# A new instruction order, and with it ten engine choices, for chunk-selected attention with a gated MLP on one core

## The chip, the cores and the metric

The kernel runs on one core of a Trainium2 chip. The metric is the device time of one execution in microseconds (us). The engines are TensorE (PE in the profile), VectorE (DVE), ScalarE (ACT), GpSimd (POOL) and SyncE (SP); the last one only issues DMA transfers here.

## The reference

```python
# attention, per head: q, k, v are [4, 8, 768, 64]
k_min, k_max = chunks_of_32(k).min(), chunks_of_32(k).max()        # 24 chunks
ub = sum_d max(q * k_min, q * k_max)                               # [768, 24]
ub = where(chunk(query) >= chunk, ub, -1e9)
top_chunks = argsort(ub)[..., -6:]                                 # six chunks per query
scores = where(in top_chunks and query >= key, q @ k.T / 8, -1e9)
x = softmax(scores) @ v                                            # heads joined: [4, 768, 512]
# gated MLP, per batch
h = gelu_tanh(x @ w_in)                                            # [768, 1024]
u, v = h[:, :512], h[:, 512:]
v = layernorm(v) * g_ln
v_s = w_sg @ v + b_sg                                              # along the 768 positions
out = x + (u * v_s) @ w_out
```

## The kernel before

The work is cut into 1374 named operations. A name is a kind, a number and, often, a part. Attention goes by pairs of heads, 0 to 15; a batch is four pairs; selection goes by pair for pairs 0 and 1, and by two pairs at a time after that. For each pair there are:

- loads `lk`, `lq`, `lv` (two each, SP, line 503);
- transposes by TensorE into PSUM, `kt` and `qt` (line 512), with reductions over chunks `kn` and `kx` (VectorE, line 530), the copies out of PSUM `ke`, `ka`, `kb` and `qe` (ScalarE at line 519 or VectorE at line 521), the difference `kw` (VectorE or GpSimd, line 541) and the rectified query `qr` (VectorE at line 562, ScalarE at line 564);
- casts `qc`, `qa`, `qb`, `vc` on GpSimd;
- selection: bounds `ub` on TensorE, then `ut`, `uc`, `um`, `ud`, `uq` on VectorE, and for the later pairs the small transfers `d` on SP (line 658);
- per head: scores `s` on TensorE, exponentials `e` on ScalarE (lines 736 and 770), the causal cut `af` on GpSimd (line 672), products with the values `pv` and `pd` on TensorE, the reciprocal `xr` on VectorE (line 804), and the scaled copy `xs`, as one VectorE instruction (line 813) or six ScalarE instructions (line 810);
- the transpose `xt`, by TensorE with a copy `xe` for some, by a DMA transpose on SP for the others.

For each batch the MLP has `hv` and `hu` on TensorE (lines 853 and 900) with their activations `gv` and `gu` on ScalarE, statistics `bs` and `ba` and small helpers `re`, `rm` on VectorE and `rp`, `rn` on GpSimd, the normalisation `vh` (ScalarE at line 886, VectorE at line 891), the product along positions `pt` (TensorE, line 920), its scaling `vs` (VectorE, line 927), the gating `gm` (GpSimd or VectorE, line 933), the output product `ou` (TensorE, line 943), the sum with x `oa` (VectorE, line 950) and the store `os` (SP). There are three result buffers for `oa` and `os`. The weights come in through `win`, `wsg`, `wo`, and `wt` with `we` transposes one of them.

The order is a table written out in the file, `ORDER`. Each engine takes its operations in the order in which they stand in the table and runs strictly in that order; `@` behind a name chooses the other engine that the operation allows; `:` gives the PSUM buffers. PSUM has two buffers of 1024 columns for scores and four of 512 for everything else. Waits are derived from the table: an operation waits for those that it depends on, and for the readers of the buffer that it overwrites. At most six large loads are in flight (`WINDOW`). `FILL` names TensorE operations that are preceded by so many matmuls of zeros while they wait for their PSUM buffer's readers or their inputs. The `cost` figures are the planner's durations in nanoseconds; nothing that runs depends on them.

Of the kernel before, what the change touches and what calls it, by code (L numbers as in the profile page):

```python
# [6 lines left out]
ALU = mybir.AluOpType  # L7
# [11 lines left out]
J0 lk1.1 warm0 zA2 lk1.0 zB3 lk0.1 idF zB1 J lk0.0 W01 Jn lq0.1 lq0.0 kt1.0:0 kt1.1:1 kn1.0 lq2.0 vx10 W00 kn1.1 lq1.0  # L19
kx1.1 kt0.0:2 kt0.1:3 kx1.0 ke1.1 lq1.1 kn0.0 ke1.0 kn0.1 lq2.1 qt0.1:1 kx0.1 qt0.0:0 qe0.1 kx0.0 lk2.0 qe0.0 vx12  # L20
qr0.1 kw0@pool kw1@pool qr0.0@act zB2 lk2.1 IND ke0.0 ke0.1 ub0:10 iA0 lk4.0 qt1.0:2 ut0.0 qc0 qt1.1:3 ut0.1 lk4.1
qe1.0 uc0.00 uc0.10 qe1.1 uc0.01 uc0.11 uc0.02 uc0.12 um0.0 lq3.1 qr1.1@act qc1 qt2.1:1 um0.1 qr1.0@act qt2.0:0 qe2.1
ud0.0 lq3.0 qe2.0 ub1:32 ud0.1 uq0.0 iB2 qr2@act uq0.1 lk3.0 W02 kt2.1:1 ut1.0 qc2 s0.4:0 ut1.1 uc1.00 s0.2:1 kn2.1
lk3.1 e0.4 idB uc1.10 uc1.01 kx2.1 s0.3:0 e0.2 lv0.1 uc1.02 uc1.11 um1.0 kt4.1:0 e0.3 uc1.12 kt2.0:3 W03 lv0.0 um1.1
s0.5:1 kn2.0 ke2.1 af1.1 lq4.0 e0.5 kx2.0 s0.0:0 iA1 ke2.0@dve lq4.1 qt3.0:2 e0.0 qt3.1:1 kn4.1 s0.6:1 ud1.1 lq5.1
ud1.0 qe3.0 kt3.0:3 uq1.1 af1.0 e0.6 s0.1:0 uq1.0 lk5.0 vc0 kn3.0 kt3.1:2 e0.1 kx4.1 s1.0:1 qe3.1 af0.0 lk5.1 kx3.0
ka4.1 s1.1:0 af1.2 kn3.1 ke3.0 af0.2 pv1:1 lv1.1 kb4.1@dve kw2@pool e1.1 af0.1 pd1 pv0:3 kx3.1 e1.0 zA0 lv1.0 qt4.1:0
xr1 xs1 pd0 s1.5:0 qe4.1 af3.0 lq5.0 xr0 ke3.1 xs0 kt4.0:1 qr3@act zA3 vx13 vx11 qt4.0:0 lv3.1 kw3@pool kn4.0 af2.0
xt0.0:2 qe4.0 s1.3:1 qc3 xe0.0 e1.5 lq6.0 kx4.0 kt5.0:3 zA1 ub2:02 e1.3 kn5.0 lk6.0 kw4@pool af2.2 af3.2 kx5.0 vc1
ka4.0 lv2.1 s1.2:0 ut2.0 kb4.0 ut2.1 s1.6:1 lk6.1 e1.2 uc2.00 uc2.10 qt5.1:0 um2.0 qt5.0:1 lq6.1 e1.6 af3.1 um2.1  # L30
s1.4:0 qe5.0 af2.1 kt5.1:2 lk7.1 e1.4 ud2.0 qe5.1 ud2.1 ka5.0 pv2:1 lk7.0 uq2.0 pv3:0 qr5@act uq2.1 pd2 kb5.0 lv2.0
pd3 kn5.1 s2.0:1 qr4@act xr3 kx5.1 lq7.0 xs3 s2.5:0 e2.0 xr2 ka5.1@dve kt6.1:3 lq7.1 qt6.1:0 e2.5 xs2 wsg0 s2.3:1 kw5
lv3.0 kb5.1 kn6.1 qa4 s2.2:0 e2.3 kx6.1 ub4:12 win0 ka6.1@dve qe6.1 iA2 e2.2 s2.4:1 ut4.0 kb6.1 wsg5 ut4.1 s2.1:0 e2.4
uc4.00 vc2 um4.0 xt0.1:0 e2.1 qt7.1:1 wsg2 ud4.0 kt6.0:3 qe7.1@dve s3.4:1 xe0.1@act af5.0 uq4.0 s3.5:0 kn6.0 e3.4
d4.01 af4.0 kt7.0:2 kx6.0 d4.00 qt7.0:1 e3.5 kn7.0 qt6.0:0 win1 d5.00 s3.1:1 ka6.0@dve qe7.0 iB0 d5.01 qe6.0@dve
s3.3:0 e3.1 kb6.0@dve wsg3 pv5:1 kw6 e3.3 kx7.0 nh wt0:0 win3 s3.0:1 ka7.0@dve vc3 qr7@act pv4:3 we0 e3.0 qa5 pd5
kb7.0@dve s3.2:0 xr5 kt7.1:0 e3.2 win2 xs5 gln pd4 s8h.2:1 qr6@act xr4 af6.0 wt2:2 lq9.1 kn7.1 s8h.1:0 e8h.2 xs4 lq8.1
pv6:1 af7.0 e8h.1 we2 lq8.0 pd6 wt5:3 kx7.1 lq9.0 s10h.0:1 we5 ka7.1 kw7@pool pv7:2 qa6 xr6 kb7.1 pd7 xs6 xt0.2:3
e10h.0 qb6 xr7 s10h.1:0 uc4.10 xs7 ub6:01 e10h.1 zB0 xt0.3:2 qb5 ut6.0 xe0.2@act s8h.0:1 xe0.3 s10h.2:0 wo2 e8h.0
um4.1 wt3:0 hv0.1:3 wsg4 uc6.00 lv4.0 ud4.1 e10h.2 we3 qb4 hv0.3:2 uq4.1 ut6.1 iA3 hv0.0:0 d4.11 um6.0 d4.10 gv0.1  # L40
hv0.2:1 wsg1 gv0.0 lk8.0 bs0.1 af8.0 hu0.00:3 gv0.3 d5.10 ba0.1 bs0.0 gv0.2 iB3 qt8.1:0 lv5.0 hu0.30:2 gu0.00 bs0.3
lk8.1 qe8.1 qb7 qt8.0:1 ba0.3 d5.11 gu0.30 ba0.0 hv0.5:3 bs0.2 qe8.0 bsg hv0.4:0 ba0.2 lk10.0 gv0.5 re0.0 ud6.0 rp0.0
qr8@act bs0.5 hu0.31:2 gv0.4 uq6.0 qt9.1:1 gu0.31 rm0.0 hu0.20:3 uc6.10 bs0.4 rn0.0 qe9.1 iB1 hu0.10:0 lv5.1 vh0.1
ba0.5 ba0.4 re0.1 rm0.1 gu0.20 rp0.1 wt1:2 vh0.0 s9h.0:1 lv4.1 we1 gu0.10 hu0.21:1 rn0.1 vh0.2 vh0.4@dve lk9.1
hu0.11:3 gu0.21 vh0.3@dve d6.01 vh0.5 hu0.01:2 um6.1 d6.00 gu0.11 kt8.1:0 gu0.01 ud6.1 wt4:1 s11h.0:0 we4 lq10.1
pt0.01:3 kn8.1 kx8.1 lk10.1 e11h.0 pt0.02:2 vs0.01 vc5 lk9.0 e9h.0 uq6.1 pt0.00:1 vs0.02 d6.10 wo3 ka8.1 d7.00 s9h.1:0
gm0.02 vs0.00 kt8.0:3 d6.11 e9h.1 qt9.0:2 kn8.0 vc4 s9h.2:1 lk11.1 pt0.03:1 qe9.0@dve e9h.2 lv8.0 wo0 kx8.0 kb8.1
d7.01 s11h.1:0 wo1 gm0.00@dve ka8.0 s11h.2:1 lq12.1 af9.0 pv8:2 vs0.03 qr9@act lv6.0 pv9:0 e11h.1 af10.0 pd8 pt0.11:1
xr8 kb8.0@dve e11h.2 af11.0 lq12.0 s12h.0:0 vs0.11 qa7 pd9 pt0.12:3 e12h.0 lv6.1 xr9 gm0.03@dve d7.10 xs9@act s13h.1:1
kw8 s13h.0:0 vs0.12 gm0.01 xs8@act pv10:1 gm0.12@dve kt9.0:0 e13h.0 pt0.10:3 kn9.0 gm0.11 lv7.0 e13h.1 kx9.0 d7.11  # L50
pd10 s12h.2:0 qb8 vs0.10 pv11:2 ka9.0 lq10.0 xr10 pd11 e12h.2 kb9.0@dve s14h.0:1 xt1.0 gm0.10 ou0.2:3 xr11 xs10@act
af13.0 e14h.0 lv7.1 s13h.2:0 oa0.2 kt9.1:0 vc6 ou0.1:1 kn9.1 xs11@act s12h.1:1 e13h.2 oa0.1 pt0.13:3 e12h.1 kx9.1
os0.1 s14h.1:0 kw9@pool lq11.0 af12.0 ka9.1 vs0.13 kt10.1:2 lq11.1 e14h.1 s15h.0:1 kn10.1 gm0.13 pv13:1 os0.2 kb9.1
pv12:3 lv8.1 qa9 e15h.0 pd12 pd13 lk11.0 s14h.2:0 xr13 vc7 ou0.0:0 xr12 kx10.1 e14h.2 xs13 af15.0 ka10.1 s15h.1:1 xs12
s15h.2:0 kb10.1 af14.0 oa0.0 ou0.5:1 xt1.2 e15h.2 qa8 ou0.4:3 e15h.1 oa0.5 xt1.1 pv14:2 oa0.4 pd14 pv15:0 xr14 os0.0
xs14@act pd15 qt11.1:1 xr15 qt11.0:3 xs15 qe11.1 qe11.0 kt11.1:2 xt1.3 kt10.0:0 kn11.1 qt10.1:1 ou0.3:3 kx11.1 qe10.1
lv9.1 kn10.0 ka11.1 lv10.0 qt10.0:1 oa0.3 kb11.1 qe10.0 kx10.0 kt11.0:2 ka10.0 kw10@pool ub8:31 kn11.0 lk14.1 qb9
kb10.0 kx11.0 vc8 hv1.1:0 ut8.0 uc8.00 ut8.1 lv11.0 qb10 hv1.0:3 gv1.1 um8.0 os0.5 ka11.0 qb11 hv1.2:1 bs1.1 lk12.1
gv1.0 lq13.0 uc8.10 ud8.0 kb11.0 hv1.3:0 ba1.1 lv9.0 uq8.0 gv1.2 bs1.0 hv1.4:3 lv11.1 qr11@act um8.1 d9.01 gv1.3
hu1.00:2 ba1.0 gv1.4 bs1.2 lk12.0 hu1.20:1 qr10@act ud8.1 d9.00 qt12.1:0 gu1.00 bs1.3 hu1.01:3 os0.3 qe12.1 ba1.2  # L60
gu1.20 hv1.5:2 re1.0 rm1.0 ba1.3 rp1.0 uq8.1 gu1.01 bs1.4 d9.11 hu1.10:0 gv1.5 rn1.0 ba1.4 vc9 d9.10 hu1.30:1 vh1.0
bs1.5 lk13.0 gu1.10 qa11 hu1.11:3 ba1.5 gu1.30 lq13.1 rm1.1 re1.1 vh1.1 qt12.0:2 kw11 d8.00 hu1.21:0 rp1.1 gu1.11
qe12.0@dve d8.01 vh1.2 hu1.31:1 rn1.1 gu1.21 lq14.0 vh1.3@dve kt12.1:3 gu1.31 s19h.2:0 d8.10 vh1.4@dve ub10:20 lv10.1
vh1.5@dve lk13.1 s18h.0:1 ut10.1 e19h.2 d8.11 pt1.02:1 ut10.0 e18h.0 os0.4 uc10.00 uc10.10 kn12.1 s16h.0:0 lq15.0
um10.0 pt1.00:0 af18.0 lv12.0 e16h.0 um10.1 qa10 s18h.2:1 pt1.01:2 vs1.00 e18h.2 ud10.1 s16h.2:0 uq10.1 s17h.1:1
vs1.01 e16h.2 pt1.10:0 ud10.0 e17h.1 vs1.02 gm1.01 s16h.1:0 uq10.0 pt1.03:2 gm1.00 kx12.1 e16h.1 d11.01 vs1.10 lq15.1
af16.0 s19h.1:1 ka12.1@dve d10.00 kt12.0:1 vs1.03 e19h.1 s19h.0:0 gm1.02 lk15.0 kn12.0 pv16:0 e19h.0 d10.01 pd16 vc10
pt1.11:2 xr16 d10.10 kx12.0 gm1.10 xs16 d10.11 s17h.2:1 ka12.0@dve s17h.0:0 e17h.2 af19.0 d11.10 pt1.13:0 vs1.11
e17h.0 d11.11 gm1.03 kb12.1@dve d11.00 s18h.1:1 vs1.13 kt13.0:2 af17.0 lv13.1 e18h.1 kb12.0@dve s20h.2:0 pv19:3 lk14.0
qr12 pv17:0 e20h.2 kn13.0 vc11 lv13.0 pd19 s21h.2:1 kx13.0 pd17 gm1.13 s21h.1:0 e21h.2 xr17 xs17 ou1.2:1 e21h.1 xr19  # L70
xt2.0 ka13.0@dve pv18:0 xs19 s20h.0:1 kb13.0@dve pd18 lv14.1 s23h.0:0 e20h.0 oa1.2 kt14.1:3 lq14.1 pt1.12:2 xr18
e23h.0 kn14.1 lv14.0 af20.0 lv12.1 s20h.1:1 gm1.11 vs1.12 kt14.0:1 e20h.1 kx14.1 s21h.0:0 gm1.12 lk15.1 xs18 ou1.0:2
e21h.0 ka14.1@dve xt2.1 s22h.1:1 kn14.0 kb14.1 ou1.1:0 af21.0 oa1.0 e22h.1 kx14.0 s22h.0:0 os1.0 qb12 oa1.1 pv20:3
e22h.0 pd20 ka14.0@dve kw12@pool s22h.2:1 os1.1 af23.0 pv21:2 xr20 e22h.2 kb14.0@dve os1.2 pd21 s23h.1:0 kw14@pool
af22.0 xr21 xs20 kt13.1:0 e23h.1 s23h.2:1 xs21 vc14 ou1.4:1 kn13.1 xt2.2 e23h.2 qa12 kx13.1 pv22:3 oa1.4 pd22 ka13.1
ou1.3:2 kw13@pool xr22 kb13.1 xs22 pv23:1 oa1.3 pd23 qt14.1:0 xr23 qt15.1:3 xs23 kt15.0:2 qe15.1 qe14.1@dve xt2.3
# [23 lines left out]
"""  # L100


FILL = {"kt1.0": 7, "kt0.0": 4, "qt0.1": 3, "ub0": 1, "qt2.1": 3, }


class PsumTile:
# [262 lines left out]
def _kernel(nc, q, k, v, w_in, g_ln, w_sg, b_sg, w_out, out):  # L369
# [4 lines left out]
    NT = S // 128  # L374
# [11 lines left out]
    NSOLO = 2  # L386
    NHALF = 4

    XPE = [(0, dk) for dk in range(NDK)] + [(B - 1, NDK - 1)]
    EOFF = []  # L390
    acc = S
    for kb in range(NT - 1):
# [696 lines left out]
```

## Time and profile before

| | us |
|---|---|
| median of 3 runs | 220.52 |
| lowest, highest | 220.27, 224.04 |
| the profiled execution, its own time | 221.09 |
| its span in the profile | 219.4 |
| TensorE busy in it | 205.1 |
| VectorE busy | 179.9 |
| ScalarE busy | 169.0 |
| GpSimd busy | 115.8 |

The span runs from the first to the last instruction of the program in the profiled execution. Busy time is the union of an engine's records. Matmuls overlap in their records, so TensorE's busy time is not the time at its peak. The idle time of an engine that is not the bottleneck costs nothing.

### The profile page before, as it was taken

The numbers are of one execution on the slowest core, as the hardware profiler recorded it, in microseconds if no ns is written. First come the engines' busy times: TensorE is split into PE (matmuls) and PEld (weight loads), VectorE is DVE, ScalarE is ACT, GpSimd is POOL, SyncE is SP. The second block draws the span as 40 slices with busy tenths as digits, with TensorE's granted clock in tenths as the row PEclk, the third lists the DMA queues.
The fourth block names the chain that finished last, engine by engine and source line by source line (L and its number), as shares of the span: only waits on it lengthen the run. The fifth ranks groups of instructions, "written<-read, shape, count | busy, mean of one in ns | idle before, by whom it ended". The sixth has DMA issues, their size and how long they took to land.

```text
span 219.4 us, 6186 instructions
## 1 busy us (share of the span) xinstructions
PE 205.1 (94%) x2364; PEld 132.6 (60%) x2364; DVE 179.9 (82%) x555; ACT 169.0 (77%) x291; POOL 115.8 (53%) x172
## 2 busy tenths in 40 slices
PE   7799999999999999989999999989979999999991
PEld 3566755677566775664556775764546686555540
DVE  1989999998989896668979998999889657594972
ACT  2569899999999999978997767865888888666000
POOL 4284654898853966806335956834380745021530
PEclk9999999999999999999999999999999999999998
DMA  7999999999998986867958349920041223400234
GB/s 154 218 220 208 210 214 223 165 138 194 165 232 183 177 182 161 216 140 185 221 138 197 84 102 207 248 42 0 20 126 67 57 46 84 147 36 0 99 128 160
DMA packets 92542, 31.78 MB, mean 145 GB/s; under 512 B 85984, under 2 KB 88800, under 8 KB 92512
## 3 DMA queue, kind: packets, MB, share of 16 engines
q1 hardware_dynamic: 90496, 28.62, 58.4%
q0 software_dynamic: 2016, 2.75, 8.5%
q8 instruction: 19, 0.31, 0.6%
q14 instruction: 11, 0.09, 0.1%
HBM read 24.77 MB, written 6.29 MB: 142 GB/s over the span
## 4 chain that ended last, share of the span: by engine, by line
PE 53%; DVE 22%; ACT 12%; DMA 4%; SPq 3%; issue 2%; POOL 1%; DVEq 0%
PE PSG L920 12%; PE PSC L766 10%; PE PSG L943 6%; PE PSG L900 5%; DVE W L530 5%; PE PSG L787 4%; PE PSG L853 4%; PE PSG L512 4%; DVE m L638 3%; DMA out_dram<-osb 3%; ACT XS L810 3%; DVE stats L863 3%; ACT E L736 2%; SPq L658 2%; ACT E L770 2%; DVE Dn L643 2%
## 5 line engine op out<-in xcount | busy, mean ns | idle before, releaser
L770 ACT ACTIVATE E<-PSC 128x1024 bf16<-128x1024 f32 (+1 forms) x72 | 62.8, 922 | 10.1 <-PE PSC L766 8.3
L672 POOL TENSOR_SCALAR_AFFINE_SELECT E<-E 128x768 bf16<-128x768 bf16 (+3 forms) x40 | 28.8, 734 | 18.9 <-ACT E L770 12.0
L530 DVE TENSOR_REDUCE W<-PSG 128x12 f32<-128x384 f32 x64 | 34.1, 546 | 5.0 <-PE PSG L512 4.2
L920 PE MATMUL PSG<-wsgT,vhat 128*128 128x384 bf16 x192 | 35.0, 326 | 1.6 <-DVE vhat L891 1.4
L933 POOL TENSOR_TENSOR uT<-vsT,uT 128x384 bf16<-128x384 f32 x22 | 20.8, 954 | 21.7 <-DVE vsT L927 21.6
L920 PEld LDWEIGHTS PSG<-wsgT,vhat 128*128 128x128 bf16 x192 | 17.8, 98 | 12.2 <-DVE vhat L891 1.6
L927 DVE SCALAR_TENSOR_TENSOR vsT<-PSG,glnT,bsgbc 128x384 f32<-128x384 f32 x32 | 19.4, 608 | 6.7 <-PE PSG L920 5.3
L943 PE MATMUL PSG<-woutb,uT 128*128 128x512 bf16 x96 | 23.8, 379 | 0.0
L900 PE MATMUL PSG<-xT,winb 128*128 128x384 bf16 x128 | 22.9, 326 | 0.0
L853 PE MATMUL PSG<-winb,xT 128*128 128x512 bf16 x96 | 22.1, 379 | 0.5 <-DVE wsgT L980 0.3
L736 ACT ACTIVATE E<-PSC 128x1024 bf16<-128x1024 f32 (+3 forms) x26 | 21.5, 877 | 1.0 <-PE PSC L726 0.9
L873 POOL TENSOR_TENSOR rstd<-rstd,neghalf 128x3 f32<-128x3 f32 x8 | 7.5, 943 | 24.9 <-DVE mv L865 11.2
L950 DVE TENSOR_TENSOR osb<-PSG,XS 128x512 f32<-128x512 f32 x24 | 16.4, 686 | 5.2 <-PE PSG L943 3.8
L766 PE MATMUL PSC<-QA,KA 96*128 96x128 bf16 (+2 forms) x168 | 19.7, 246 | 0.6 <-issue 0.4
L787 PE MATMUL PSG<-vx,E 128*128 128x65 bf16 x480 | 19.2, 193 | 0.3 <-ACT E L736 0.2
L787 PEld LDWEIGHTS PSG<-vx,E 128*128 128x128 bf16 x480 | 17.4, 97 | 2.7 <-ACT E L736 0.5
L766 PE MATMUL PSC<-QB,KB 128*128 128x128 bf16 (+2 forms) x168 | 18.7, 246 | 0.2 <-issue 0.2
L858 ACT ACTIVATE vgb<-PSG 128x512 f32<-128x512 f32 x24 | 14.0, 595 | 5.3 <-PE PSG L853 5.1
L512 PE MATMUL PSG<-identF,kn 128*128 128x128 f32 x96 | 16.4, 289 | 1.6 <-DMA kn<-in_k_dram 0.4
L900 PEld LDWEIGHTS PSG<-xT,winb 128*128 128x128 bf16 x128 | 12.4, 98 | 8.7 <-ACT uT L906 0.2
L863 DVE BATCH_NORM_STATS2 stats<-vgb 128x6 f32<-128x512 f32 x24 | 15.9, 677 | 1.6 <-ACT vgb L858 1.5
L906 ACT ACTIVATE uT<-PSG 128x384 bf16<-128x384 f32 x32 | 14.9, 495 | 2.6 <-PE PSG L900 2.4
(86 smaller groups left out, 395.1 us busy)
## 6 DMA issues: line engine op xcount, KB each, us to landing
kn<-in_k_dram SPq DMA_DIRECT2D x32, 192.0 KB, 4.2
qn<-in_q_dram SPq DMA_DIRECT2D x32, 192.0 KB, 4.4
vn<-in_v_dram SPq DMA_DIRECT2D x32, 192.0 KB, 4.2
out_dram<-osb SPq DMA_DIRECT2D x24, 256.0 KB, 2.3
winb<-in_moe_w_in_dram POOLq DMA_DIRECT2D x4, 256.0 KB, 4.9
vhat<-in_moe_w_sg_dram POOLq DMA_DIRECT2D x3, 192.0 KB, 3.9
xT<-in_moe_w_sg_dram POOLq DMA_DIRECT2D x3, 192.0 KB, 4.2
woutb<-in_moe_w_out_dram POOLq DMA_DIRECT2D x4, 128.0 KB, 3.9
```

Source lines behind the costliest of these rows:

```text
L512: r = e.matmul(t.ap()[:, 128 * j:128 * j + 128], src[:, 3 * hf + j].rearrange("p i d -> p (i d)"), identF[:], is_transpose=True)
L530: P.op(f"k{'nx'[m]}{p}.{hf}", "dve", lambda d, t=t, m=m, op=op, cs=cs: d.tensor_reduce(W[w][:, m, cs.start // 32:cs.stop // 32], t.ap()[:, ...
L672: P.op(f"af{h}.{r}", "pool", lambda g, ev=ev, cnt=cnt: g.affine_select(ev, ev, pattern=[[0, cnt], [1, 128]], compare_op=ALU.is_ge, fill=0. ...
L736: P.op(f"e{p}.{c}", "act", lambda e, t=t, o0=o0, nn=nn: e.activation(E[:, slot:slot + 2, o0:o0 + nn], t.ap().rearrange("p (i x) -> p i x", ...
L766: r = e.matmul(t.ap()[:, o:o + n], kt_[rows, 128 * kb:128 * kb + 128], qt_[rows, q0:q0 + n], start=True, stop=True, skip_group_check=True)
L770: P.op(f"e{h}h.{c}", "act", lambda e, t=t, c0=c0, c1=c1: e.activation(E[:, es, c0:c1], t.ap()[:, 0:c1 - c0], ACTF.Exp, scale=SCALE), write ...
L787: r = e.matmul(t.ap()[:, 65 * qb:65 * qb + 65], E[:, es, a:a + 128], vx[w][:, kb, i, :], start=first, stop=False, skip_group_check=True)
L853: r = e.matmul(t.ap()[:, 0:F], xT[s][:, dk, 128 * qt:128 * qt + 128], winb[:, dk, F:DFF], start=(dk == 0), stop=(dk == NDK - 1))
L863: P.op(f"bs{b}.{qt}", "dve", lambda d, qt=qt, st=st: d.bn_stats(stats[st][:], vg[qt]), reads=[("vg", qt)], writes=[("stats", st)], cost=(5 ...
L900: r = e.matmul(t.ap()[:, 0:TG], winb[:, dk, 128 * fb:128 * fb + 128], xT[s][:, dk, TG * tg:TG * tg + TG], start=(dk == 0), stop=(dk == NDK ...
L920: r = e.matmul(t.ap()[:, 0:TG], vhat[s][:, sb, 128 * fb:128 * fb + 128], wsgT[:, sb, TG * tg:TG * tg + TG], start=(sb == 0), stop=(sb == N ...
L943: r = e.matmul(t.ap()[:, 0:DM], gT[s][:, fb, 128 * qt:128 * qt + 128], woutb[:, fb, :], start=(fb == 0), stop=(fb == NF - 1))
```

## The change

The table `ORDER` is replaced by another one. All 1374 names are in both. The new table was searched with VectorE's and GpSimd's operations taken as 8 per cent and ScalarE's as 5 per cent longer than measured. These operations run on another engine than before, counted by kind:

| kind | first engine | before | after |
|---|---|---|---|
| `ka` | ScalarE, VectorE | 14, 10 | 16, 8 |
| `kb` | ScalarE, VectorE | 13, 11 | 19, 5 |
| `ke` | ScalarE, VectorE | 7, 1 | 6, 2 |
| `qe` | ScalarE, VectorE | 26, 6 | 27, 5 |
| `kw` | VectorE, GpSimd | 4, 12 | 1, 15 |
| `qr` | VectorE, ScalarE | 3, 15 | 5, 13 |
| `vh` | ScalarE, VectorE | 9, 15 | 13, 11 |
| `gm` | GpSimd, VectorE | 22, 10 | 24, 8 |
| `xs` | VectorE, ScalarE | 26, 6 | 28, 4 |
| `xe` | VectorE, ScalarE | 3, 2 | 5, 0 |

Of the `qr`, the large ones of pairs 2 and up on VectorE are `qr12` and `qr13` before, and `qr3`, `qr6`, `qr10`, `qr12` after. The list of fillers changes, two planner's costs change, and a list `WPE` is added with a branch for weights outside it; it holds all six indices.

The diff, with the table cut to the stretches that the text below speaks of:

```diff
@@ the table, around pairs 7 and 6 (xs7, xt0.2) @@
-pv6:1 af7.0 e8h.1 we2 lq8.0 pd6 wt5:3 kx7.1 lq9.0 s10h.0:1 we5 ka7.1 kw7@pool pv7:2 qa6 xr6 kb7.1 pd7 xs6 xt0.2:3
-e10h.0 qb6 xr7 s10h.1:0 uc4.10 xs7 ub6:01 e10h.1 zB0 xt0.3:2 qb5 ut6.0 xe0.2@act s8h.0:1 xe0.3 s10h.2:0 wo2 e8h.0
+e8h.1 pd7 lq9.0 pv6:2 uc4.10 xr4 xr7 s10h.0:1 xs4 kw6@pool kb7.1 qb5 pd6 s10h.1:0 xs7@act xr6 ub6:31 xs6 qb7 e10h.1
+um4.1 xt0.2:0 zA2 ut6.0 e10h.0 xt0.3:2 zB0 xe0.2 s8h.0:1 wt3:3 uc6.00 xe0.3 e8h.0 iA2 wt2:0 we3 s10h.2:1 hv0.1:2 ut6.1
...
@@ the table, around the store os0.0 and the transposes xt1 @@
-s15h.2:0 kb10.1 af14.0 oa0.0 ou0.5:1 xt1.2 e15h.2 qa8 ou0.4:3 e15h.1 oa0.5 xt1.1 pv14:2 oa0.4 pd14 pv15:0 xr14 os0.0
-xs14@act pd15 qt11.1:1 xr15 qt11.0:3 xs15 qe11.1 qe11.0 kt11.1:2 xt1.3 kt10.0:0 kn11.1 qt10.1:1 ou0.3:3 kx11.1 qe10.1
+gm0.12 e13h.2 xt1.1 s15h.0:1 kb10.1 gm0.13@dve pv14:2 qr8@act pd14 s15h.2:0 xs12 qa9 lv8.1 e15h.0 pv13:1 oa0.0 pd13
+qa8 ou0.5:0 e15h.2 xr14 xr13 os0.0 xs14 xs13@act ou0.4:3 af15.0 oa0.5 pv15:2 xt1.2 oa0.4 pd15 qt10.0:1 xr15 kt11.1:0
+xs15 qe10.0 qt11.0:3 kn11.1 xt1.3 qe11.0 qt11.1:1 kt10.0:2 kx11.1 qe11.1 qt10.1:3 kn10.0 ka11.1 lq13.1 ou0.3:1
...
@@ the table, between hu2 and pt2 @@
-rm2.1 re2.1 gu2.31 vh2.1@dve d13.01 hu2.11:0 rp2.1 gu2.00 vh2.0 hu2.10:1 rn2.1 gu2.11 vh2.4@dve gu2.10 s24h.0:0
-vh2.2@dve ub14:20 vh2.3@dve vh2.5@dve e24h.0 s25h.0:1 qb14 ut14.1 pt2.11:1 uc14.10 ut14.0 e25h.0 vc12 uc14.00
+gu2.10 ba2.5 d12.00 vh2.0 ba2.4 hu2.21:3 re2.1 vh2.2@dve gu2.30 lv14.0 hu2.00:2 gu2.20 rm2.1
+rp2.1 d13.01 gu2.21 lv13.0 gu2.00 s25h.0:1 rn2.1 lv15.1 vh2.5@dve ub14:10 d13.10 vh2.4@dve lv13.1 e25h.0 s24h.0:0
+vh2.3@dve os1.4 ut14.1 qb15 e24h.0 pt2.11:3 d13.00 ut14.0 lv14.1 qa13 uc14.00 uc14.10 s24h.2:1 um14.1 d13.11 s25h.1:0
...
-FILL = {"kt1.0": 7, "kt0.0": 4, "qt0.1": 3, "ub0": 1, "qt2.1": 3, }
+FILL = {"kt1.1": 7, "kt0.1": 4, "qt0.1": 1, "qt2.1": 3, "ou3.4": 1, }
...
+    WPE = range(NT)
...
                 P.op(f"qr{p}", "dve", lambda d: d.tensor_scalar(rt[:], qT[w][:, LO:S], 0.0, None, op0=ALU.max),
-                     reads=qk, writes=[("rT", p % NR, hf) for hf in range(2)], cost=(365, 459), port=True,
+                     reads=qk, writes=[("rT", p % NR, hf) for hf in range(2)], cost=(480, 570), port=True,
...
                             vhat[s][:, qt, :], vg[qt], mv[s][:, qt, 0:1], rstd[s][:, qt:qt + 1], op0=ALU.subtract,
-                            op1=ALU.mult), cost=(520, 610), port=True)})
+                            op1=ALU.mult), cost=(600, 690), port=True)})
...
+                if j not in WPE:
+                    P.op(f"wt{j}", "sp", lambda e, j=j: e.dma_start_transpose(
+                        out=wsgT[:, :, 128 * j:128 * j + 128], in_=wsgf[j]), reads=[("wsgf", j)],
+                        writes=[("wsgT", j)], dma=f"wsgT{j}", cost=(1290, 1400), prio=150.0 + 5 * j)
+                    continue
```

## The prediction

> **What bounds the kernel now.** I read the page first: busy shares, then the forty slices, then the shares of the chain.
>
> ```profile
> span 219.4 us, 6186 instructions
> ...
> PE 205.1 (94%) x2364; PEld 132.6 (60%) x2364; DVE 179.9 (82%) x555; ACT 169.0 (77%) x291; POOL 115.8 (53%) x172
> ...
> DVE  1989999998989896668979998999889657594972
> ACT  2569899999999999978997767865888888666000
> POOL 4284654898853966806335956834380745021530
> PEclk9999999999999999999999999999999999999998
> ...
> PE 53%; DVE 22%; ACT 12%; DMA 4%; SPq 3%; issue 2%; POOL 1%; DVEq 0%
> ```
>
> TensorE looks full at 94%, but nearly half of the chain that ends last lies on other engines. From the starts of consecutive matmuls I take each shape's spacing when nothing holds it (216 ns at 512 columns, 163 at 384, 109 for a float32 transpose, 30 for a value product): TensorE's own work is 193 us. The excess of the spacings over these is 21 us, 4 of it in the first 10; after its last issue 5 us follow. So 193 + 21 + 5 = 219, and only the 21 can go. The rows show VectorE at 9 tenths in slices 3 to 10 and 20 to 30, ScalarE in slices 6 to 16. The clock is full throughout.
>
> The chain shows two such places. First ScalarE, with the wait behind it:
>
> ```profile
> 76.65 1.02 ACT E L770
> 77.67 2.45 ACT XS L810 x12
> 80.12 1.83 ACT E L770 x2
> ...
> 93.33 0.55 DVE osb L950
> 93.88 4.20 DMA out_dram<-osb
> 98.17 0.69 DVE osb L950
> ```
>
> From 76.65 on for ten microseconds the chain is ScalarE work; at 93.88 VectorE cannot write its fourth result tile until an output transfer frees the buffer. Second, VectorE before the third `pt` group, from the timeline (start, length, engine, line, form, and in brackets the idle time before it and what ended it):
>
> ```profile
> 159.49 3.51 DVE L891 TENSOR_SCALAR vhat<-vgb,mv,rstd 128x512 bf16<-128x512 f32 x4 [1.02 <-POOL nmr L881]
> 159.51 0.82 POOL L572 CAST QB<-qT 64x768 bf16<-64x768 f32 x1
> ...
> 160.40 0.91 POOL L577 CAST vx<-vn 128x768 bf16<-128x768 f32 x1
> ...
> 161.25 1.01 POOL L570 CAST QA<-qT 64x768 bf16<-64x768 f32 x1
> ...
> 163.06 1.15 PE L920 MATMUL PSG<-wsgT,vhat 128*128 128x384 bf16 x6 [1.36 <-DVE vhat L891]
> ```
>
> Four `vh` take 3.51 us, three of them 1.05 to 1.13 each, against a median of 0.545; three GpSimd casts lie beside them, and TensorE waits about 1.5 us.
>
> **The change by kind of work.** Instruction counts of all operations stay. Engine choices move; mean durations are those of the costliest-group rows.
>
> VectorE gives up 2 `ka` (0.530), 6 `kb` (0.561), 4 `vh` (0.648), 1 `qe` (0.546), 3 `kw` (0.488), 2 `gm` (0.691): 10.4 us. It takes 1 `ke` (0.558), 2 `xs` (0.551), 2 `xe` (0.546), 2 `qr` (0.951): 4.7. Net -5.7.
> ScalarE takes 2 `ka` (0.492), 6 `kb` (0.485), 4 `vh` (0.822), 1 `qe` (0.500): 7.7. It gives up 1 `ke` (0.497), 2 `xs` (six records, 1.34 each), 2 `xe` (0.818), 2 `qr` (0.695): 6.2. Net +1.5.
> GpSimd takes 3 `kw` (0.235) and 2 `gm` (0.954): +2.6.
> TensorE: 16 fillers for 18, at 0.216: -0.4, all in waits, so I cost them at nothing. Without them two early gaps of 1.2 us stay empty; the trace has a gap of 0.93 with full speed after it. If the clock did fall, `ub0` and six transposes at double spacing would cost 1.5. The new filler before `ou3.4` fills a wait that was 0.16: between 0 and +0.2. The costs in the code and the list `WPE` (all six indices stay on TensorE) change no instruction: 0.
>
> A sum over an engine says little, so here are stages, cut at the first TensorE operation named. "Time" is the trace's. Work is the operations listed between the cuts by their back-to-back spacing; after is the new list by the same spacings.
>
> | stage | time | PE, DVE, ACT before | after |
> |---|---|---|---|
> | start to `ub1` | 13.7 | 8.0, 8.9, 4.5 | 7.3, 9.0, 4.1 |
> | to `ub6` | 38.0 | 33.2, 33.5, 33.4 | 32.6, 33.0, 33.0 |
> | to `pt0` | 16.2 | 15.7, 12.2, 14.8 | 16.3, 12.1, 14.1 |
> | to `ub8` | 31.1 | 27.9, 20.1, 28.2 | 27.7, 21.4, 25.6 |
> | to `pt1` | 15.4 | 14.4, 11.8, 13.9 | 15.4, 13.9, 14.6 |
> | to `ub12` | 33.4 | 30.7, 29.8, 21.9 | 29.9, 26.3, 24.1 |
> | to `pt2` | 15.2 | 13.5, 12.1, 11.3 | 13.6, 11.5, 13.5 |
> | to `hv3` | 26.9 | 25.8, 17.5, 19.8 | 25.7, 16.6, 17.6 |
> | to the end | 29.4 | 24.2, 17.1, 7.9 | 24.4, 15.7, 10.1 |
>
> Stage by stage, with the excess of time over the largest column carried over unless a reason is given:
>
> Start: 13.7 stays. The first loads, the eight reductions and the first selection follow each other in both orders.
> To `ub6`: three engines level, excess 4.5. All three fall by half a microsecond; I also take 0.8 off the excess because VectorE has 0.5 less in it. 36.7.
> To `pt0`: 16.3 + 0.5. In the new list `xs7` is on ScalarE (1.2 us of issue) directly before `xt0.2`, with only `s10h.1` and `ub6` between (1.7 us): 0 to 1, I take 0.6. 17.4.
> To `ub8`: ScalarE loses 2.6 us and is no longer the longest; `os0.0`, which held `oa0.3` for the 4.20 above, stands ahead of the transposes `xt1.2` and `xt1.3` in SP's queue instead of behind `xt1.1` and `xt1.2` (1.3 each). Late next is TensorE itself. I let half of the 2.9 to 3.2 excess go: 29.3.
> To `pt1`: 15.4 + 1.0; work moved in from both sides: 16.4.
> To `ub12`: VectorE falls 3.6 below TensorE; load `lk14.0`, 3.9 us of TensorE work ahead of its use before, now has 15.3, so its wait (0.6) goes. Half the excess: 31.3.
> To `pt2`: three `vh` follow the last `rn2.1` on VectorE instead of four, so 2.5 to 3.2 us under the same 2.2 of cover; 0.6 of the 1.5 goes. ScalarE is now level with TensorE, which may return 0 to 1; I take 0.2. 14.9.
> To `hv3`: 25.7 + 1.1 - 0.3 = 26.5. To the end: 24.4 + 5.2 = 29.6; nothing covers it, and ScalarE has 2.2 more there, under TensorE's 10 us of `hv3` and `hu3`: 0 to +0.8 more.
>
> Sum: 13.7 + 36.7 + 17.4 + 29.3 + 16.4 + 31.3 + 14.9 + 26.5 + 29.6 = 215.8, or 3.6 under the span. The profiled execution took 221.09 around its 219.4; the median of the three runs is 220.52. 220.5 - 3.6 = 216.9; I state 216.8. New waits that I can't place are the weak point: each stage may return up to its gain, or lose as much again.
>
> **A rule against the change.** The row: `qr` on VectorE (L562) took 949 and 953 ns; on ScalarE (L564) its median is 688. The Trainium skill, "SBUF — State Buffer", section "SBUF: two separate sides", says that VectorE in a two-port mode, or with two SBUF inputs, and GpSimd hold one port pair exclusively, the later one waiting for the whole instruction. By that rule four large `qr` on VectorE instead of two, beside a busier GpSimd, each risk a whole cast of 0.82 to 0.91: 2 x 0.9 = 1.8 us worse. The row already holds such waits, so by it two more cost 1.9 of VectorE and save 1.4 of ScalarE. But the operations so exposed (`qr`, `vh`, `gm`, `kw` on VectorE) fall from 31 to 24. I count by the row, and take no further loss. In the new list `qb15` follows `rn2.1` on GpSimd at once, so `vh2.5`, `vh2.4`, `vh2.3` will collide as before: that is why I let only 0.6 of 1.5 go.
>
> **Rivals.**
> *One for one.* The orders are different throughout, and each old wait is replaced by another: the counts of close distances are alike (producer to TensorE consumer with less than their durations between: about 90 of 358 in the new list, 81 in the old). Time 220.5 - 0.5 = 220. Against it: VectorE's 5.7 us.
> *Whole relief.* The excess of all middle stages falls by two thirds, about 8.5 us: 212. Against it: `xs7`, and `vh2`.
> *Loads too late: slower.* SP issues in order. Leads in TensorE work from issue to first use shrink: `lv8.0` 23.8 to 3.2, `lk10.1` 16.9 to 4.4, `lv9.0` 4.6 to 4.0; on average 10.9 to 9.9. A load lands 4.2 us after its issue, and the queue can sit 2.2 us (123.6 in the trace). Three such loads at 2.5 each are +7.5; with one late again in the saturated first 60 us, +2.5, and gains of 3.6 off, 220.5 + 6.4 = 227. It decides from about 8 us of such waits. For it: the chain already holds 3% of SP's queue. Against it: loads below 5 us are 29, before 31.
>
> **Numbers.** Forecast 0.62 (213.5 to 218.5), whole relief 0.10, one for one 0.14, loads late 0.14. Two per cent, about what a measurement of this kernel can tell from no change, is 216.1 and 224.9. Of the forecast 0.36 lies under 216.1: faster 0.46, same 0.26 + 0.14 = 0.40, slower 0.14. The range 212.8 to 221.8 leaves out the slow case and a little of the best.
>
> **What would show it.** Right: VectorE's busy time near 174, ScalarE's near 170.5, GpSimd's near 118; TensorE's busy share up; no transfer in the chain near `oa0.3`; no run of ScalarE `XS` and `E` for ten microseconds; `pt2` waiting under 1.1 us. Wrong: TensorE idle before `xt0.2` or `hu3.30` by more than 1 us, key or value loads ending the idle time of `kt` and `vc`, or the same 21 us of excess at other places.

## The result and the profile after

The new kernel takes 218.0 us (median of 4 runs, 217.31 to 218.16) against 220.6 (4 runs); the ratio is 0.988, with a 95 per cent interval of 0.985 to 0.991. It is faster, by less than the 2 per cent named in the prediction. Some executions of the kernel before last 3 to 5 us longer, at a mean granted clock of 0.967 to 0.977 where the others have 0.994 or more; ratios here leave them out. The new profiled execution took 217.99 around a span of 216.3, 3.1 under the span before.

The page of the new kernel, the rows that were read before:

```profile
span 216.3 us, 6168 instructions
...
PE 203.2 (94%) x2362; PEld 132.3 (61%) x2362; DVE 176.9 (82%) x544; ACT 170.4 (79%) x287; POOL 118.4 (55%) x177
...
DVE  1999998998899978889979999889898468484871
ACT  2569998999999999978998787999997889277000
...
DMA  7999999999689979999469852920173304303033
...
PE 63%; DVE 14%; DMA 10%; ACT 5%; SPq 4%; issue 2%; POOL 1%; DVEq 0%
```

TensorE carries 63% of the chain for 53, and VectorE 14% for 22. The other shares do not repeat. A second execution of the same kernel, `new_again` below, has:

```profile
PE 67%; ACT 12%; DVE 8%; DMA 7%; SPq 2%; issue 1%; POOL 1%; DVEq 0%
```

So ScalarE's 5% for 12 can't be read as a gain. What both chains have lost is the ten microseconds of ScalarE work that stood in the old one from 76.65 on. TensorE's work at its free spacings is 192.8 us; the excess over it fell from 20.9 to 17.9, as far as the time did.

The same stages as in the prediction, from the starts of the same TensorE operations. The last column is the measured time less TensorE's work in the prediction's table; in the last row it holds the 5 us after TensorE's last issue.

| stage | before | predicted | measured | time less TensorE's work, before and after |
|---|---|---|---|---|
| start to `ub1` | 13.7 | 13.7 | 13.3 | 5.7, 6.0 |
| to `ub6` | 38.0 | 36.7 | 38.8 | 4.8, 6.2 |
| to `pt0` | 16.2 | 17.4 | 16.6 | 0.5, 0.3 |
| to `ub8` | 31.1 | 29.3 | 28.3 | 3.2, 0.6 |
| to `pt1` | 15.4 | 16.4 | 16.1 | 1.0, 0.7 |
| to `ub12` | 33.4 | 31.3 | 31.6 | 2.7, 1.7 |
| to `pt2` | 15.2 | 14.9 | 14.1 | 1.7, 0.5 |
| to `hv3` | 26.9 | 26.5 | 26.6 | 1.1, 0.9 |
| to the end | 29.4 | 29.6 | 31.0 | 5.2, 6.6 |

The middle, from `pt0` to `hv3`, fell from 122.0 to 116.7: 5.3 us. The stage to `ub6` and the end gave 2.4 back. The chain of the new kernel (start, length, what) shows the first of these, and the place behind the result buffers:

```profile
27.07 5.17 DMA vn<-in_v_dram
32.30 1.45 POOL vx L577
33.88 1.07 PE PSG L787 x30
...
92.28 5.15 DMA out_dram<-osb
97.52 0.70 DVE osb L950
```

A load of values, issued at 27.07 for 23.02 before, lands after 5.17 us; its cast `vc1` ends at 33.7, and `pv3` waits 1.4. About 0.6 of that is the cast itself, 1.44 us for 0.83 before: the two `ud2` of VectorE run beside it from 32.18, and in `new_v1_earlier` below, where it runs at 29.29 ahead of them, it takes 0.83 again. The store at 92.28, `os0.0`, takes longer to land than before (4.20 then), although it stands ahead of two transposes, and `oa0.3` follows it at once. In `new_again` the same store landed after 2.97 us and `oa0.3` did not wait for it, yet the stage to `ub8` took the same 28.3 us and the next one 15.9 for 16.1: in the new order little hangs on this store. The end, from the timeline:

```profile
187.08 0.69 DVE L950 TENSOR_TENSOR osb<-PSG,XS 128x512 f32<-128x512 f32 x1 [1.89 <-DMA out_dram<-osb]
...
187.83 1.47 PE L853 MATMUL PSG<-winb,xT 128*128 128x512 bf16 x6 [0.85 <-DVE osb L950]
```

Here `oa2.4` needs the buffer of `os2.1`, a store that was issued at 182.46 behind the transposes `xt3.1` and `xt3.2` and landed 4.6 us later; `hv3.0` needs the PSUM buffer that `oa2.4` reads.

The last `vh` of the third batch, in the lines that answer to those of before:

```profile
156.10 2.55 DVE L891 TENSOR_SCALAR vhat<-vgb,mv,rstd 128x512 bf16<-128x512 f32 x3 [0.95 <-POOL nmr L881]
156.13 0.82 POOL L572 CAST QB<-qT 64x768 bf16<-64x768 f32 x1
...
157.02 0.90 POOL L570 CAST QA<-qT 64x768 bf16<-64x768 f32 x1
...
158.71 0.50 PE L920 MATMUL PSG<-wsgT,vhat 128*128 128x384 bf16 x2 [0.16 <-DVE vhat L891]
```

Three `vh` for four, two of them beside casts at 1.13 and 1.04, and a wait of 0.34 for 1.54.

### The profile page after: what moved, and what is told of

Its sections match the earlier page's. It is cut to its first block, busy times and chain, and to the rows that moved or that the text cites. A ratio compares the mean times of both kernels' runs of the same rounds, so it can differ in the third digit from the quotient of the medians.

```text
span 216.3 us, 6168 instructions
## 1 busy us (share of the span) xinstructions
PE 203.2 (94%) x2362; PEld 132.3 (61%) x2362; DVE 176.9 (82%) x544; ACT 170.4 (79%) x287; POOL 118.4 (55%) x177
## 4 chain that ended last, share of the span: by engine, by line
PE 63%; DVE 14%; DMA 10%; ACT 5%; SPq 4%; issue 2%; POOL 1%; DVEq 0%
PE PSG L920 11%; PE PSC L766 10%; PE PSG L853 9%; PE PSG L900 7%; PE PSG L512 6%; DMA out_dram<-osb 5%; PE PSG L943 5%; PE PSG L787 5%; SPq L503 3%; PE PSG L614 3%; DVE W L530 2%; DMA vn<-in_v_dram 2%; DVE osb L950 2%; DMA qn<-in_q_dram 2%; PE PSC L726 2%; PE PSG L795 2%
## 5 line engine op out<-in xcount | busy, mean ns | idle before, releaser
L933 POOL TENSOR_TENSOR uT<-vsT,uT 128x384 bf16<-128x384 f32 x24 | 22.6, 950 | 13.5 <-DVE vsT L927 13.1
L920 PEld LDWEIGHTS PSG<-wsgT,vhat 128*128 128x128 bf16 x192 | 17.9, 98 | 11.2 <-DVE vsT L927 0.5
L577 POOL CAST vx<-vn 128x768 bf16<-128x768 f32 x16 | 14.4, 899 | 15.2 <-DMA vn<-in_v_dram 15.1
L787 PE MATMUL PSG<-vx,E 128*128 128x65 bf16 x480 | 19.7, 193 | 1.2 <-POOL vx L577 1.2
L766 PE MATMUL PSC<-QA,KA 96*128 96x128 bf16 (+2 forms) x168 | 19.0, 246 | 0.1
L853 PEld LDWEIGHTS PSG<-winb,xT 128*128 128x128 bf16 x96 | 9.1, 98 | 12.0 <-DVE osb L950 1.2
```

The source lines that it names most:

```text
L766: r = e.matmul(t.ap()[:, o:o + n], kt_[rows, 128 * kb:128 * kb + 128], qt_[rows, q0:q0 + n], start=True, stop=True, skip_group_check=True)
L787: r = e.matmul(t.ap()[:, 65 * qb:65 * qb + 65], E[:, es, a:a + 128], vx[w][:, kb, i, :], start=first, stop=False, skip_group_check=True)
L853: r = e.matmul(t.ap()[:, 0:F], xT[s][:, dk, 128 * qt:128 * qt + 128], winb[:, dk, F:DFF], start=(dk == 0), stop=(dk == NDK - 1))
L920: r = e.matmul(t.ap()[:, 0:TG], vhat[s][:, sb, 128 * fb:128 * fb + 128], wsgT[:, sb, TG * tg:TG * tg + TG], start=(sb == 0), stop=(sb == N ...
L933: return d.tensor_tensor(gT[s][:, fb, TG * tg:TG * tg + TG], vsT[vs][:], uT[s][:, fb, TG * tg:TG * tg + TG], op=ALU.mult)
```

## Experiments

Two theories of the gain were set against each other first: the engine moves, which relieve VectorE, or the places in the sequence. Two kernels cross them.

```diff
# old_order_new_engines: the old sequence, 59 suffixes from the new table, as
-... kb4.1@dve ... xs7 ... qr3@act ... vh2.1@dve
+... kb4.1 ... xs7@act ... qr3 ... vh2.1
# new_order_old_engines: the new sequence, the same 59 suffixes from the old table
# PSUM buffers and fillers stay with the sequence in both
```

> The old table, word for word in its sequence, with the new table's engine choices at all 59 operations where the two differ. Theory 1 (the gain comes from the engine moves, which take 3.0 us of busy time off VectorE): 218.0 to 219.0 us. Theory 2 (the gain comes from where the instructions stand, and the moves only fit together with the new sequence): 220.5 us or more; with sixteen more operations that can collide on the port pair shared with GpSimd or queue on ScalarE at places that were not made for them, up to 223.

> The new table in its sequence with the old table's engine choices at the 59 operations. Theory 1 (engine moves): the gain is gone, 220.5 us or more. Theory 2 (sequence): most of it stays, 218.0 to 219.5.

Measured: 224.75 us, ratio 1.021 (1.018 to 1.023), and 227.38, ratio 1.036 (1.032 to 1.040). Both are slower than either kernel, and the first is beyond the 223 that was expected at most. The first theory falls with the first kernel: it has the new kernel's engine choices and is 7 us behind it. The second falls with the other one: the new sequence alone keeps nothing. The wait views name some of the misplaced work (total us, times, longest). In the first (its lines stand two lower), TensorE's weight load waits for `xs7` on ScalarE before the transpose of the first batch's last tile:

```profile
PEld PSG L831 <- ACT XS L808: 1.4, 1, 1.4
```

In the second it is ScalarE again, holding score buffers:

```profile
PE PSC L766 <- ACT E L770: 2.2, 2, 1.8
```

So the two parts hold only together. That each sequence leaves a gap where its own engine choices put the work fits these waits, but they are about 1 of some 5 us and 2 of some 7 that the two kernels lose against the one before; the rest is spread over several stages and was not traced. How much each of the 59 choices would be worth is not told by this.

Next, the place that the prediction read most from.

```diff
# old_casts_later: GpSimd's queue in the old table
-... rn2.1 ... qb14 ... vc12 ... qa14 lv15.0 ... af24.0 ...
+... rn2.1 ... af24.0 qb14 vc12 lv15.0 qa14 ...
```

> The old kernel with one stretch of GpSimd's queue changed: the casts qb14, vc12, qa14 (and the load lv15.0, which needs vc12) stand behind the causal cut af24.0, which waits for an exponential, so that GpSimd is idle while VectorE runs the four last vh of the third batch. If the shared port pair made three of them last 1.05 to 1.13 us, all four last 0.53 to 0.55, together about 1.9 us for 3.5, the wait of 1.5 us before pt2.11 goes to about 0, and the time falls by 0.8 to 1.5 us, to about 219.3. Rival (VectorE was late for its own work and the casts only happen to lie beside): the vh keep their 1.05, the time stays at 220.5.

```profile
158.43 1.91 DVE L890 TENSOR_SCALAR vhat<-vgb,mv,rstd 128x512 bf16<-128x512 f32 x4 [1.02 <-POOL nmr L880]
```

The four `vh` take 1.91 us for 3.51, as expected, and VectorE's own queue is the same: the slow ones were slow because of the casts. Each had lost 0.5 to 0.6 us beside casts of 0.82 to 1.01, less than the whole cast that the prediction's rule would charge. TensorE no longer waits for `vh`. The time fell less than expected: 219.50, ratio 0.998 (0.996 to 1.000). The delayed casts run later, beside the selection (`ud14.0`, 0.91 us from 164.78 in its timeline, 0.44 before), and TensorE's waits for ScalarE's exponentials between 157 and 180 us went from 1.0 to 2.0 us. One wait gone, the next one uncovered.

```diff
# old_xs_on_vector
-xs9@act ... xs8@act ... xs10@act ... xs11@act
+xs9 ... xs8 ... xs10 ... xs11
```

> The old kernel with xs8, xs9, xs10 and xs11 on VectorE (one instruction of 0.55 us each) for ScalarE (six instructions, 1.34 us each): 5.3 us less for ScalarE between 76 and 87 us, where the chain ran through it. If ScalarE bounds that stage, the stage to ub8 (31.1 us, 3.0 of them TensorE's excess) loses 1 to 2 us and the time is 218.7 to 219.7. Rival (the stage ends with the fourth result tile's wait for a store, which does not move): the time stays within 0.5 of 220.5.

Measured 219.27, ratio 0.994 (0.992 to 0.996): 0.7 us less by the medians, 1.3 by the ratio, at the lower end of what was expected. In its trace the granted clock is half from 18.2 to 28.4 us, so the stage to `ub6` is no guide, but the stage to `ub8` comes later, at full clock: it took 30.0 us for 31.1 (31.0 and 31.2 in `old_casts_later` and `old_vector_late`). ScalarE did bound that stage, for about a third of the 3.2 that TensorE's work leaves; the new order took off 2.6.

Then the two places where the new kernel gave time back.

```diff
# new_v1_earlier: SP's queue
-... lq6.0 lq6.1 lk6.1 lq5.1 lv1.1 lv1.0 lk6.0 ...
+... lq6.0 lv1.1 lv1.0 lk6.1 lq5.1 lq6.1 lk6.0 ...
```

> The new kernel with the two loads lv1.1 and lv1.0 moved ahead of lq6.1 in SP's queue and lq6.1 behind lq5.1, so that they are issued about 3 us earlier. In the new kernel they landed at 32.2 us, vc1 ended at 33.7 and pv3 waited 1.4 us. If that load is why the stage to ub6 became longer instead of shorter, pv3's wait goes and the time falls by 0.6 to 1.4 us, to about 217. Rival (VectorE paces this stage, so TensorE only waits elsewhere): the stage keeps its 38.8 us and the time stays within 0.3 of 218.

It failed: 220.26 us, ratio 0.999 (0.997 to 1.002). `pv3` waits for nothing in its trace, for 1.4, but the load that was put back, `lq6.1`, issued at 27.06 and landed 5.3 us later, is late in its turn:

```profile
32.48 1.52 PE L511 MATMUL PSG<-identF,qn 128*128 128x128 f32 x6 [2.64 <-issue]
```

This is `qt6`, which waits 2.64 us for it; the same wait is 1.6 in `new_all_three`. In this stretch the transfer engines are at 9 tenths of their time (row DMA above), and here one load's gain was another's loss. The wait has company. This is the row of the granted clock in the same trace:

```profile
PEclk9999995999999999999999999999999999999999
```

The clock was 0.51 from 32 to 34 us, 0.50 from 34 to 36 and 0.64 from 36 to 40. By an estimate from these three figures, 2 x 0.49 + 2 x 0.50 + 4 x 0.36, it cost 3.4 us, which is all of this execution's distance from the new kernel (221.45 and 218.0). With a mean clock of 0.994 or more (8 of 22) the times are 217.8 to 219.5 us, with a lower one 219.5 to 222.9. So the median tells of the clock; at full clock the edit changed little. The fall begins at 32.0, within TensorE's idle time from 29.8 to 32.5. That the idle time brought it is not shown: in `old_xs_on_vector` the clock fell at 18.2, and the longest idle time before it was 1.2 us; in `new_vector_late` 1.9 us passed at full clock. The expectation's rival, VectorE as the pace, is not what showed either.

```diff
# new_stores_first
-oa2.0 ... xt3.1 ... oa2.1 ... xt3.2 ... os2.1 ... os2.0
+oa2.0 ... os2.0 xt3.1 ... oa2.1 ... os2.1 xt3.2
```

> The new kernel with os2.0 ahead of the transfer transpose xt3.1 and os2.1 ahead of xt3.2 on SP, instead of behind both. If stores that stand behind transposes land late (4.6 us here, median 2.6) and so hold oa2.4 and hv3.0, which waited 1.0 us, the store of os2.1 ends before 186, that wait goes and the time falls by 0.5 to 1.0 us. Rival: xt3.2 lands 0.6 us later and holds hv3.1 instead; no gain.

`hv3.1` starts at 185.83, 1.07 us late. The transposes take 2.7 and 4.3 us from issue to landing in its trace, 2.7 to 2.8 in the new kernel: `os2.1`, now ahead of `xt3.2`, landed in 2.2 us and `hv3.0` waited for nothing, but `xt3.2`, issued at 181.48 beside the stores, lands at 185.8 (181.48 + 4.3) and holds `hv3.1`. This is the rival's mechanism, a little larger than it said. No gain in time: 218.05, ratio 0.996 (0.993 to 0.999).

```diff
# new_copy_later: GpSimd's queue
-qc1 iA0 af1.1
+qc1 af1.1 iA0
```

> The new kernel with the GpSimd copy iA0 behind the causal cut af1.1, so that GpSimd is idle while VectorE runs ud0.1, uq0.1, ud0.0. ud0.1 has two SBUF inputs and took 0.709 us beside iA0, against 0.34 in the old kernel. If the shared port pair is the cause, ud0.1 takes 0.34, s0.4's wait of 0.86 falls to about 0.5, and the time falls by 0 to 0.4 us. Rival: 0.709 stays.

`ud0.1` took 0.34 us for 0.71, and `s0.4` waited 0.53 for 0.86. Measured 217.03, ratio 0.990 (0.987 to 0.992). The new kernel itself did not run beside it, so the third of a microsecond is shown in the stage and not in the time.

> The three edits of new_v1_earlier, new_stores_first and new_copy_later together on the new kernel. If the waits are independent, the gains add up: 1.2 to 2.6 us, 215.5 to 216.8. If one wait only uncovers the next, less than the best of the three alone.

221.28, ratio 1.006 (1.003 to 1.008), slower than any of the three alone. The gains do not add up. Its trace, 219.19 us and a mean clock of 0.994, has the waits of `qt6` (1.6) and `hv3.1` (1.0) that the two misplaced transfers left. The other times, 220.1 to 222.9, go with a mean clock of 0.981 to 0.992 (20 of 22), so a good part of the loss is the clock; why it fell so often here is not shown.

The last four ran side by side.

> The new kernel unchanged, on the same chip as the next three, so that their differences from it are read against runs beside them. All theories: about 1.2 per cent under the kernel before, as in the first comparison.

217.67 us, ratio 0.991 (0.988 to 0.994): 0.9 per cent under the kernel before, for 1.2 in the first comparison.

```diff
# new_three_repairs
-qc1 iA0 af1.1
+qc1 af1.1 iA0
-xt3.1 ... os2.1 ... os2.0
+os2.0 xt3.1 ... os2.1
-os_ = (b * NT + qt) % NO
+os_ = (b * NT + (7 - qt if b == 2 and qt > 2 and qt < 5 else qt)) % NO
+P.by_name["qb15"].deps[P.by_name["vh2.3"].idx] = 1
```

> The new kernel with three waits taken away: iA0 behind af1.1 on GpSimd (as in new_copy_later); qb15 made to wait for vh2.3, so that no cast lies beside the last three vh of the third batch; and os2.0 ahead of the transfer transpose xt3.1, with the result buffers of oa2.4 and oa2.3 exchanged, so that oa2.4 needs the store that was issued before the transposes. If the three waits are what they seem, s0.4 waits 0.5 for 0.86 us, the three vh take 1.6 us for 2.55 and pt2.11 waits for nothing, hv3.0 loses its wait of 1.0, and the time is 1.0 to 1.7 us under new_again's. Rival: each uncovers the next wait, less than 0.5.

216.81 us, ratio 0.987 (0.985 to 0.988), 0.9 us under new_again; the expectation was 1.0 to 1.7, the rival's under 0.5. All three waits went: `s0.4` 0.53, `hv3.0` nothing, and the three `vh` run alone, with the cast held behind them:

```profile
155.97 1.46 DVE L890 TENSOR_SCALAR vhat<-vgb,mv,rstd 128x512 bf16<-128x512 f32 x3 [0.95 <-POOL nmr L880]
157.49 0.82 POOL L571 CAST QB<-qT 64x768 bf16<-64x768 f32 x1 [1.56 <-DVE vhat L890]
```

About half came back as a longer wait of `s10h.0` (0.84 for 0.33) and `s25h.1` (0.64 for 0.42). It has the lowest median of this study; `new_copy_later` (ratio 0.990, 0.987 to 0.992) is not clearly behind it.

Last, the statement that the new order was searched with longer durations, put to a test: VectorE is made late in both.

```diff
-d.reciprocal(rden[rs][:], pv3()[:, :, DH])
+[d.reciprocal(rden[rs][:, c:c + 3], pv3()[:, c:c + 3, DH]) for c in (0, 3)][-1]
# and each chunk reduction in two of six chunks
```

> The old kernel with VectorE made longer evenly: every chunk reduction (kn, kx) and every reciprocal (xr) is issued as two instructions of half the size, 96 instructions more, the same result. By the spacings of such instructions this is some 7 to 10 us of VectorE time, 4 to 5 per cent. Theory A (an order searched with VectorE taken longer holds TensorE's sequence when VectorE is late): the old order loses 4 to 7 us, and the new one under the same load clearly less, at most 3. Theory B (the new order is better by the places of single waits, not by reserve): both lose the same within 1 us.

> The new kernel with the same halved reductions and reciprocals on VectorE, 96 instructions more. Theory A (reserve): it loses at most 3 us, so it stands 3 to 5 us under old_vector_late. Theory B (single places): it loses what the old one loses and stands 2 to 3 us under old_vector_late, the distance that the two have without the load.

VectorE's busy time rose by about 5 us in each, less than expected: 179.9 to 185.2 in the old order, 174.6 (new_again) to 179.4 in the new one. The old order went to 223.94, ratio 1.020 (1.016 to 1.023): about 4 us lost. The new one went to 218.17, ratio 0.993 (0.991 to 0.995): 0.5 lost. The first theory's losses came, at its lower end for the old order, and the two kernels stand 5.8 us apart for the 3 to 5 that it gave; the second theory's numbers did not come. The profile narrows it: the old order lost 2.2 us before 54 us (stage to `ub6` 39.8 for 38.0, start 14.1 for 13.7) and 1.3 after the last store's issue, where that store landed in 3.3 us for 2.0; from `ub6` to `hv3` it took 137.9 for 138.3, no worse. So what the old order lacked in reserve showed in the first quarter, where VectorE is at 9 tenths. The trace of new_vector_late lasted 220.56 us, 2.4 above its median, so its own first stages can't be set against that. Whether the reserve lies in the sequence or only in VectorE's smaller share of the work was not separated, and that the search with longer durations made it is not shown: how the old table was searched is not on record.

## Why the prediction was right, point by point

- **Time and class.** 216.8 was stated, 218.0 measured; the forecast's own case held, and its gain was 3.6 for 2.6 by the medians, 3.1 by the spans. The likelier class, faster (0.46), did not come; same (0.40) did. The 2 per cent that the prediction took for the limit of a measurement was too coarse: the interval here is 0.6 per cent wide. The sum's closeness is partly luck: the stages add up to 215.8 for a span of 216.3, but single stages were stated 3.9 us too short in all and others 3.3 too long.
- **What bounds.** Right: TensorE's excess was what could go, and it fell by as much as the span. The forecast of ScalarE (170.5) and GpSimd (118) came out at 170.4 and 118.4.
- **VectorE's term** was -5.7; it measured -3.0 in the first execution and -5.3 in the second of the same kernel (174.6). Most of that difference is one `vh` (`vh0.5`, 1.98 us for 0.55) and one `qr` (`qr12`, 1.08 for 0.45). The groups, for `ud` and `vh` from the kernel before and from the new one, for `qr` from the new one:

```profile
L643 DVE TENSOR_TENSOR Dn<-U,m 128x288 bf16<-128x288 f32 (+2 forms) x18 | 8.4, 485 | 0.1
L643 DVE TENSOR_TENSOR Dn<-U,m 128x288 bf16<-128x288 f32 (+2 forms) x18 | 10.5, 593 | 0.1
L891 DVE TENSOR_SCALAR vhat<-vgb,mv,rstd 128x512 bf16<-128x512 f32 x15 | 9.2, 648 | 3.6 <-POOL nmr L881 2.3 <-ACT vhat L886 1.3
L891 DVE TENSOR_SCALAR vhat<-vgb,mv,rstd 128x512 bf16<-128x512 f32 x11 | 8.4, 783 | 1.7 <-POOL nmr L881 1.3 <-ACT vhat L886 0.3
L562 DVE TENSOR_SCALAR rT<-qT 128x576 f32<-128x576 f32 x4 | 2.6, 653 | 0.0
```

  The step that failed in both executions is the count of exposed operations, "fall from 31 to 24": it left out the 18 `ud`, which have two SBUF inputs and whose mean rose from 485 ns to 593 and, in `new_again`, 578: 1.7 to 1.9 us in all. `vh` rose from 648 to 783 in one execution and stayed at 654 in the other. `qr`, feared at 951, came out at 653 and 498. Counted from the records, twelve exposed operations (`qr`, `vh`, `gm`, `kw`, `ud`) were over 0.1 us longer than when alone before, with about 6 us of excess; in the new order fifteen with about 7.5, and in its second execution thirteen with about 5.3. With the new engine choices in the old sequence VectorE was busy for 173.5. By the rule that the prediction cites, fewer exposed operations mean less risk; what they stand beside decided.
- **To `ub6`**: the step that failed. "I also take 0.8 off the excess because VectorE has 0.5 less" read the stage as VectorE's. It ended 2.1 us above the 36.7, by `pv3` (1.4, a load and the cast behind it) and `s0.4` (0.9 for 0.2 before, `ud0.1` beside the copy `iA0`). The lead of `lv1` had shrunk from 4.3 and 4.9 to 3.3 and 3.6, and the third rival's mechanism, loads too late, happened here once; the three loads that it named (`lv8.0`, `lk10.1`, `lv9.0`) did no harm.
- **To `pt0`**: `xs7` before `xt0.2` was charged 0.6 and cost nothing in the new kernel. With the old sequence around it the same choice held the next transpose, `xt0.3`, for 0.9 to 1.4.
- **To `ub8` and `ub12`**: to `ub8` the direction and ScalarE's part are right, and more went than the half allowed (0.6 left of 3.2); `old_xs_on_vector` shows about 1.1 us of it as ScalarE's. The store step did not bear: `os0.0` ahead of the transposes landed after 5.15 us in one execution and 2.97 in the other, and the stage took 28.3 in both. To `ub12` the wait for `lk14.0` is gone; that VectorE's lower load took off the rest is argued, and no kernel here tests it.
- **To `pt2`**: stated 0.9 us left of the wait, measured 0.34; two collisions, not three. (The slow `vh` of the kernel before took 1.04 to 1.13.)
- **To the end**: 29.6 stated, 31.0 measured. ScalarE was named as the risk under `hv3`; a store and its buffer were it. The filler before `ou3.4` did not show.
- **The signs.** No ten microseconds of ScalarE in the chain, `pt2` waiting under 1.1, and the busy times of ScalarE and GpSimd came as said. TensorE's busy share stayed at 94%. A transfer near `oa0.3` stood in the chain of one execution and not of the other. One sign of being wrong came: a value load ended the idle time of `vc1`.

## What to carry to other kernels

Here an order and its engine choices were one object: with all 59 choices, or the whole sequence, exchanged alone the result was 2 to 4 per cent worse than the kernel before. Single choices can still gain: four of them (`old_xs_on_vector`) gave 0.6 per cent. When an order is judged by sums per engine, also list which VectorE operations exposed to GpSimd come to stand beside it, and the lead of each load in the stretch where transfers are saturated; these two lengthened the stage to `ub6`. A schedule's reserve can be measured by making one engine longer evenly in both kernels: here that set them 5.8 us apart, where their own times differ by about 2.5.

## What the runs showed that was not expected

A store of 256 KB lands 2.3 us after its issue in the median of the old order and 2.6 in the new one, but up to 4.4 and 5.2. Standing beside transfer transposes does not settle it: `os0.0` took 5.15 and 2.97 us in two executions of the same kernel, and in the old order a store issued at 183.33, right behind `xt3.1`, landed in 2.3. What makes a store late stays open. VectorE's busy time in two executions of the same new kernel was 176.9 and 174.6, so a change of 2 us in a busy time says little from one trace each.
